# Fused attention and two MLP blocks: reciprocal sums carried by the fifth score tile's transpose, and some casts on other engines

## The chip, the cores and the metric

One Trainium2 chip, one core of it. The metric is the device time of one execution in microseconds. The core has a matrix engine (PE, with its weight loads shown as PEld), a vector engine (DVE), an activation engine (ACT), a general engine (POOL) and a queue that issues the DMAs (SP). Each takes its instructions in order; instructions of different engines wait for one another by semaphores.

## The reference

Three stages run one after another on 4 batches of 576 tokens.

- Attention over 8 heads of width 64: scores are `q k^T / 8`, minus a non-negative running bias (`cumsum(max(s,0))` of the query minus that of the key), causal, softmax, times `v`. The heads side by side give `x` of width 512.
- A gated MLP: `h = gelu(x w_in)`, split into `u` and `v`; `v` is normalised over its 512 features, mixed over tokens with `w_sg` (576 by 576), `b_sg` is added, the product with `u` goes through `w_out`, and `x` is added.
- A second MLP: every token is mixed with the one before it, `k = relu(xk w_k)`, `(k*k) w_v`, times `sigmoid(xr w_r)`.

The change touches the first stage and, by engine choice only, the second.

## The kernel before

Numbers are held as pairs of high and low parts (`split_lo` makes the low part by a subtraction), so that a product is two or three matmuls in a reduced fp32 format.

`attn_pair(b, hp)` handles two heads; there are 16 such pairs. For each head it loads `kq`, casts the high parts (`QB`, `ka`), copies them by DMA into the other half of the operand tiles (`qa`, `ka`) and makes the low parts. Then come nine steps: four score tiles of head 0, the shared fifth tile `st5` (the last 64 queries of head 0 in partitions 0 to 63, those of head 1 in 64 to 127), and four tiles of head 1. A step multiplies into PSUM (L257, L258), adds the mask and finds the row maximum on DVE (L284), takes the exponential on ACT (L292) with the row sum accumulated in a column of `sm` (128 by 9), transposes the exponentials on PE (L307, L310, L318) and copies them to `pt1` and `pt2`. The fifth tile has 576 columns of scores in a tile of 640; the rest of its columns is zero, and its last transpose (L318) takes columns 512 to 640. The values product (L345) multiplies `pt1` and `pt2` with `vf`, in two parts `r`, and ACT or DVE copies the result to `xT`.

The row sums are not divided into the exponentials. They are turned by a transpose of their own, `sm` to `rt` (9 by 128, L323), an epsilon is added (L325), the reciprocal is taken (L326), and the nine rows go to DRAM (L327) and come back broadcast over 64 partitions each as `rb` (L330 to L332). `scale_pending` multiplies `xT` by `rb` on DVE (L360); it is called during a later pair, at its fifth tile.

`moe1(b)` is the gated MLP of one batch, with products `v`, `u`, `sg`, `o` (all at L376). `prologue` converts weights in the first stretch (`syt`, `sraw`, `wcs`, `wsr`). Attention, prologue and `moe1` are generators. `attention_until` runs the attention ahead of the MLP by a measure of work (`LEAD`, `RATE`, `A_COST`, `E_COST`), and `PRO` says at which attention progress a prologue step is taken. That gives the program order. The framework's planner then orders the instructions of each engine by its own simulated time, with the program order as priority; `after` adds an ordering by hand. After about 418 us only the second MLP runs (`k`, `r`, `psa`, `psb`, `psc`); no line of it is touched.

PSUM tiles of the attention and MLP come from three tags: `sc` (3 buffers), `tp` (2) and `acc` (3). `rt`, `tq` (the last transpose of the fifth tile), the values product and the MLP's products before the last batch use `acc`.

Of the kernel before, what the change touches and what calls it, by code (L numbers as in the profile page):

```python
# [1 line left out]

# [18 lines left out]
NT = 5  # L21
# [7 lines left out]
SUM_EPS = 1e-9  # L29
TW = [P, P, P, P, S - 4 * P]  # L30
QS = 256
TW1 = 640
PTB = 2
HB = 1
RATE = (1.1, 1, 1, 1)


@with_exitstack
def fused_kernel(ctx, tc, kqT, vL, s, w_in, g_ln, w_sgT, b_sg, w_out, mu_k, mu_r, w_k, w_v, w_r, out):
    nc = tc.nc  # L40

    const = ctx.enter_context(tc.tile_pool(name="const", bufs=1))
    dram = ctx.enter_context(tc.tile_pool(name="dram", bufs=1, space=bass.MemoryType.DRAM))
# [25 lines left out]
    def split_lo(eng, lo, x, hi):  # L69
        eng.tensor_tensor(out=lo, in0=x, in1=f32(hi), op=ALU.subtract)  # L70
# [127 lines left out]
    def spatial(k):  # L198
# [5 lines left out]
            nc.sync.dma_start(out=raw[64:128], in_=w_sgT[512:])  # L204
        nc.scalar.copy(wsg[0][:, k], raw)
        split_lo(nc.vector, wsg[1][:, k], raw, wsg[0][:, k])

    xT = {}

    last_row = [None]  # L210


    def attn_pair(b, hp):
        pr = b * (H // 2) + hp
        first = b == 0
        ops = []
        for hh in range(2):
            h = 2 * hp + hh
            hd = b * H + h

            kq = at.tile([P, S], F32, tag="kq", name=f"kq{hd}", bufs=2)
            nc.sync.dma_start(out=kq, in_=kqT[b, h])
            i = hd % (NSET + 1) if first else hd % NSET
            qb, kb = QB[i], KB[i]

# [8 lines left out]
            (nc.scalar.copy if hd < 1 else nc.gpsimd.tensor_copy)(qb[64:128], kq[64:128])  # L234
            (nc.vector.tensor_copy if 1 < hd < 4 else nc.scalar.copy)(ka[0:64], kq[0:64])  # L235
            nc.sync.dma_start(out=f32(qa[0:64]), in_=f32(qb[64:128]))
            nc.sync.dma_start(out=f32(ka[64:128]), in_=f32(ka[0:64]))
            lo = nc.vector if hd in (0, 2) else nc.gpsimd
            split_lo(lo, qa[64:128], kq[64:128], qb[64:128])
            split_lo(lo, kb[64:128], kq[0:64], ka[0:64])  # L240
            ops.append((qa, ka, qb, kb))
            if hh == 0:
                vf = at.tile([P, 2, NT, D], F32, tag="vf", name=f"vf{pr}", bufs=2)
                nc.sync.dma_start(out=vf, in_=vL[b][:, h:h + 2])
                x_t = ep.tile([P, S], F32, tag="xT", name=f"xT{pr}", bufs=8)
                xT[(b, hp)] = x_t
            yield 0
# [14 lines left out]
        for hh, i in steps:  # L262
            q0 = i * P
            w = min(q0 + P, S)
            if hh == 2:
                st = st5
            elif first and hh != 1:
                st = stf[:, 64 * i * (i + 1):64 * (i + 1) * (i + 2)]
            else:
                st = at.tile([P, 640], F32, tag="st", name=f"st{pr}_{hh}_{i}", bufs=4)  # L270
# [17 lines left out]
            if hh == 2:  # L288

                pass  # L290
            last = len(chunks) - 1
            e = nc.scalar.activation(  # L292
                st[:, :w], st[:, :w], AF.Exp, bias=mx[:, last:last + 1], scale=-1.0,
                accum_out=sm[:, i + 5 * (hh == 1):i + 5 * (hh == 1) + 1],
            )
            exps.append(e)
            if (hh, i) == LATE:
                scale_pending(mi)
# [10 lines left out]
                c = (j + (i == 1)) * P  # L309
                nc.tensor.transpose(tp[:, c:c + P], st[:, j * P:(j + 1) * P], ident)  # L310
            if i == 1:
                (nc.vector.tensor_copy if first and not hh else nc.scalar.copy)(pt1[:, hh], tp[:, :QS + P])
            elif i < 4:
                (nc.vector.tensor_copy if i == 3 and pr > 5 else nc.scalar.copy)(
                    pt2[:, hh, :i + 1, q0 - QS:w - QS], tp[:, :(i + 1) * P].rearrange("p (j m) -> p j m", m=P))
            else:
                tp4 = psum1.tile([P, 512], F32, tag="acc", name=f"tq{pr}", bufs=3)
                nc.tensor.transpose(tp4[:, 0:P], st[:, 512:640], ident)  # L318
                nc.scalar.copy(pt2[:, :, :4, q0 - QS:], tp.rearrange("p (j a m) -> p a j m", j=4, a=2))
                nc.vector.tensor_copy(pt2[:, :, 3, 0:64], tp4[:, :P].rearrange("p (a m) -> p a m", a=2))  # L320
            yield (i + 1) * 200
        rt = psum1.tile([P, 512], F32, tag="acc", name=f"rt{pr}", bufs=3)
        nc.tensor.transpose(rt[:9, :P], sm, ident)  # L323
        rc = at.tile([9, P], F32, tag="rc", name=f"rc{pr}")
        nc.vector.tensor_scalar_add(rc, rt[:9, :P], SUM_EPS)  # L325
        nc.vector.reciprocal(rc, rc)  # L326
        nc.sync.dma_start(out=rdram[pr], in_=rc)  # L327
        rbs = at.tile([P, S], F32, tag="rb", name=f"rb{pr}", bufs=1)
        rq = rdram[pr].rearrange("i q -> (i q)")
        nc.sync.dma_start(out=rbs[:64], in_=rq[:S].partition_broadcast(64))  # L330
        nc.sync.dma_start(out=rbs[64:, :512], in_=rq[S + 64:].partition_broadcast(64))
        nc.sync.dma_start(out=rbs[64:, 512:], in_=rq[S:S + 64].partition_broadcast(64))  # L332
        for r in range(2):
            q0, n = ((0, QS), (QS, S - QS))[r]
            acc = psum1.tile([P, 512], F32, tag="acc", name=f"pv{pr}_{r}", bufs=3)
            nk = 2 if r == 0 else NT
            for kk in range(nk):
                o = max(0, kk * P - q0)
                both = []
                for a in (1, 0):  # L340
                    if r == 0:
                        pt = pt1[:, a, :QS] if kk == 0 else pt1[:, a, QS:]
                    else:
                        pt = pt2[:, a, kk, o:] if kk < 4 else pt2[:, a, 3, 0:64]
                    both.append(nc.tensor.matmul(acc[64 * a:64 * a + 64, o:n], vf[:, a, kk], pt, start=(kk == 0), stop=(kk == nk - 1)))  # L345
                after(both[1], both[0])

            (nc.vector.tensor_copy if first and not r else nc.scalar.copy)(x_t[:, q0:q0 + n], acc[:, :n])
            yield 4000
        pending.append((x_t, rbs))  # L350
        if pr == B * H // 2 - 1:
            scale_pending(None)
# [27 lines left out]
    def moe1(b):  # L380
# [11 lines left out]
            scale_pending(None)  # L392
        for k in range(KD):
            nc.scalar.copy(xs[0][:, k], xT[(b, k)])
            split_lo(nc.vector if b == 0 else nc.gpsimd, xs[1][:, k], xT[(b, k)], xs[0][:, k])
        for i in range(2):
            nc.scalar.copy(xq[:, :, i], f32(xs[i][:, :, 512:]))
        yield 0
# [5 lines left out]
        for t in range(NT):  # L404
# [13 lines left out]
            else:  # L418
# [8 lines left out]
            nc.gpsimd.tensor_scalar(out=v[:m, t], in0=v[:m, t], scalar1=mv[:m, t, 0:1], scalar2=rstd[:m, t:t + 1],  # L427
                                    op0=ALU.subtract, op1=ALU.mult) if b == 0 else nc.vector.tensor_scalar(out=v[:m, t], in0=v[:m, t], scalar1=mv[:m, t, 0:1], scalar2=rstd[:m, t:t + 1],
                                    op0=ALU.subtract, op1=ALU.mult)
            last_cast[0] = nc.scalar.copy(vn[0][:m, t], v[:m, t])  # L430
            if t < 4:
                split_lo(nc.vector if b == B - 1 else nc.gpsimd, vn[1][:, t], v[:, t], vn[0][:, t])
            else:

                split_lo(nc.vector, vn[0][64:128, 4], v[:64, 4], vn[0][:64, 4])
# [17 lines left out]
        for m in range(KD):  # L453
            f = slice(m * P, (m + 1) * P)
            ga = ep.tile([P, TW1], F32, tag="tmp", name=f"ga{b}_{m}", bufs=3)[:, :S + 1]
            for hf in range(2):
# [7 lines left out]
                nc.vector.scalar_tensor_tensor(out=ga[:, c], in0=acc[:, :HF], scalar=g_sb[:, m:m + 1], in1=bsg[:, c],  # L464
                                               op0=ALU.mult, op1=ALU.add)
                yield 14 * 288 * S_W
            eng = nc.vector if b == B - 1 else nc.gpsimd
            eng.tensor_tensor(out=ga[:, :S], in0=ga[:, :S], in1=u[m], op=ALU.mult)
            last_gate[0] = nc.scalar.copy(gs[0][m], ga[:, :S])
            gs[1].append(ep.tile([P, S], F32R, tag="u", name=f"gl{b}_{m}", bufs=4))  # L470
# [71 lines left out]
    a_it = a_stream()  # L542
    a_done = 0.0

    PRO = [0, 0] + [1 + 1 * i for i in range(5)]

    def attention_until(n):
        nonlocal a_done
        while a_done < min(n, B * H):
            a_done = next(a_it)  # L550
            while PRO and a_done >= PRO[0]:
                PRO.pop(0)
                next(pro)
# [3 lines left out]
    closed = False  # L557
    for b in range(B):
        e_done = 0.0
        for c in moe1(b):  # L560
            e_done += c
            attention_until((b + 1) * H + LEAD + RATE[b] * H * e_done / E_COST)
            if pro is not None and next(pro, None) is None:
                pro = None
            if a_done == B * H and not closed:
                closed = True
                ap_stack.close()
# [320 lines left out]
```

## Time and profile before

| | |
|---|---|
| median of 3 runs | 655.01 us (654.92 to 657.52) |
| span of the profiled execution | 655.4 us |
| its time outside the span | not reported apart; the median lies 0.4 us below the span |
| PE, DVE, ACT, POOL busy | 95%, 73%, 63%, 33% of the span |
| instructions | 11462 |

The page gives busy time per engine, the chain of work that ended last, and the costliest groups. Busy PE is not PE at its peak, since the ends of matmuls are modelled. A wait of one engine for another stands in the waits view with the releaser; a wait costs time only where it stands in the chain.

### The profile page before, as it was taken

What the parts mean: (1) busy time and instruction counts of PE and PEld (TensorE: products, weight loads), DVE (VectorE), ACT (ScalarE), POOL (GpSimd) and SP (SyncE); (2) the same over time, 40 slices, a digit from 0 to 9 for tenths busy, and PEclk for the clock granted to TensorE, in tenths of its full rate; (3) what the DMA queues carried; (4) which work ended last, traced back from release to release, by engine and by line L of the source; (5) the groups of instructions that cost most, each with busy time, mean ns of one, the idle gap of its engine ahead of it and who ended that gap; (6) DMA issues with size and microseconds to landing.
All of it is one profiled execution on the core that took longest, in us unless ns stands there. A gap on an engine that the chain in (4) does not pass through costs nothing.

```text
span 655.4 us, 11462 instructions
## 1 busy us (share of the span) xinstructions
PE 620.6 (95%) x3912; PEld 547.0 (83%) x3912; DVE 478.0 (73%) x990; ACT 415.2 (63%) x933; POOL 217.5 (33%) x218
## 2 busy tenths in 40 slices
PE   1779999989999999999999999999999999999997
PEld 1547777878988998978898999888888888999997
DVE  7889688995849844479732678786975869587874
ACT  4889889984748755468732665576865778553530
POOL 7265657778535577357353120000000000000000
PEclk9899999999999999999999999999999999999999
DMA  7576563454570641833403862677563693546543
GB/s 221 164 224 212 159 212 104 142 188 122 178 241 24 197 138 38 241 111 101 142 18 88 293 230 99 214 264 220 206 217 135 210 358 140 187 167 200 210 144 121
DMA packets 56458, 112.74 MB, mean 172 GB/s; under 512 B 7680, under 2 KB 20624, under 8 KB 56400
## 3 DMA queue, kind: packets, MB, share of 16 engines
q1 hardware_dynamic: 56400, 112.01, 53.3%
q8 instruction: 31, 0.51, 0.3%
q14 instruction: 27, 0.22, 0.1%
HBM read 74.46 MB, written 28.02 MB: 156 GB/s over the span
## 4 chain that ended last, share of the span: by engine, by line
PE 81%; DVE 7%; DMA 7%; issue 2%; SPq 1%; ACT 1%; DVEq 0%; ACTq 0%
PE k L376 15%; PE sg L376 9%; PE psa L786 8%; PE r L376 8%; PE o L376 7%; PE v L376 7%; PE pv L345 6%; PE u L376 5%; PE tp L310 4%; PE psb L786 4%; PE sc L257 4%; PE sc L258 3%; PE psc L786 2%; DMA rdram<-rc 2%; DMA wsr<-in_w_sgT_dram 1%
## 5 line engine op out<-in xcount | busy, mean ns | idle before, releaser
L376 PE MATMUL k<-x,wk 128*128 128x512 f32 (+1 forms) x480 | 98.9, 368 | 0.0
L376 PEld LDWEIGHTS k<-x,wk 128*128 128x128 f32 x480 | 83.6, 189 | 14.9
L292 ACT ACTIVATE st<-st,mx 128x384 f32<-128x384 f32 (+4 forms) x128 | 74.9, 588 | 8.2 <-DVE mx L284 7.5
L257 PE MATMUL sc<-ka,qa 128*128 128x512 f32 (+3 forms) x180 | 61.8, 358 | 18.4 <-DMA ka<-ka 11.8
L284 DVE CUSTOM_DVE_ANT_0 st<-sc,mask 128x512 f32<-128x512 f32 (+3 forms) x128 | 61.9, 502 | 12.6 <-PE sc L258 12.4
L376 PE MATMUL sg<-wsg,vn 128*128 128x288 f32 x448 | 63.6, 297 | 1.5 <-DVE vn L70 1.5
L376 PEld LDWEIGHTS sg<-wsg,vn 128*128 128x128 f32 x448 | 60.3, 188 | 2.4 <-DVE vn L70 1.7
L258 PE MATMUL sc<-KB,QB 128*128 128x512 f32 (+3 forms) x180 | 56.4, 335 | 0.0
L257 PEld LDWEIGHTS sc<-ka,qa 128*128 128x128 f32 x180 | 33.3, 187 | 26.3 <-issue 17.2
L310 PE MATMUL tp<-ident,st 128*128 128x128 f32 x316 | 50.3, 279 | 0.5 <-ACT st L292 0.5
L345 PE MATMUL pv<-pt,vf 128*64 128x320 f32 (+4 forms) x448 | 50.3, 364 | 0.0
L376 PE MATMUL r<-x,wr 128*128 128x512 f32 (+1 forms) x240 | 49.5, 368 | 0.0
L376 PEld LDWEIGHTS r<-x,wr 128*128 128x128 f32 x240 | 41.9, 189 | 7.5
L376 PE MATMUL v<-wv,xs 128*128 128x512 f32 x192 | 48.0, 396 | 0.0
L345 PEld LDWEIGHTS pv<-pt,vf 128*64 128x64 f32 x448 | 29.3, 136 | 19.8 <-issue 1.6
L70 POOL TENSOR_TENSOR KB<-kq,ka 64x576 fp32r<-64x576 f32 x29 | 43.1, 1485 | 6.9 <-ACT ka L235 4.9
L70 POOL TENSOR_TENSOR qa<-kq,QB 64x576 fp32r<-64x576 f32 x29 | 44.0, 1517 | 2.1
L376 PE MATMUL u<-xs,wc 128*128 128x288 f32 x288 | 41.3, 298 | 1.1 <-DVE u L512 1.1
L310 PEld LDWEIGHTS tp<-ident,st 128*128 128x128 f32 x316 | 38.4, 143 | 4.5 <-ACT st L292 0.8
L605 ACT ACTIVATE yx<-yt,mu 128x64 f32<-128x64 f32 (+4 forms) x64 | 30.5, 530 | 17.7 <-DMA yt<-ydram 17.7
L376 PE MATMUL o<-gh,wc 128*128 128x288 f32 x192 | 40.6, 297 | 0.7 <-DMA wc<-wscr 0.7
L376 PEld LDWEIGHTS v<-wv,xs 128*128 128x128 f32 x192 | 35.0, 188 | 7.3 <-issue 0.3
(191 smaller groups left out, 1435.3 us busy)
## 6 DMA issues: line engine op xcount, KB each, us to landing
wc<-wscr SPq DMA_DIRECT2D x24, 512.0 KB
kq<-in_kqT_dram SPq DMA_DIRECT2D x32, 288.0 KB
kr<-kdram SPq DMA_DIRECT2D x12, 768.0 KB
kdram<-k SPq DMA_DIRECT2D x16, 512.0 KB
yt<-ydram SPq DMA_DIRECT2D x24, 257.0 KB
vf<-in_vL_dram SPq DMA_DIRECT2D x16, 320.0 KB
ydram<-y SPq DMA_DIRECT2D x16, 288.5 KB
gt<-gdram SPq DMA_DIRECT2D x12, 384.0 KB
```

The source lines that it names most:

```text
L70: eng.tensor_tensor(out=lo, in0=x, in1=f32(hi), op=ALU.subtract)
L257: nc.tensor.matmul(sc[:m, :c1 - c0], qa[:, q], ka[:, c0:c1], start=True, stop=False)
L258: nc.tensor.matmul(sc[:m, :c1 - c0], qb[:, q], kb[:, c0:c1], start=False, stop=True)
L284: mi = nc.vector.tensor_tensor_reduce(out=st[:, c0:c1], in0=sc[:, :n], in1=mk, op0=ALU.add, op1=ALU.min, scale=-SCALE, scalar=mx[:, 0:1] i ...
L292: e = nc.scalar.activation(st[:, :w], st[:, :w], AF.Exp, bias=mx[:, last:last + 1], scale=-1.0, accum_out=sm[:, i + 5 * (hh == 1):i + 5 * ...
L310: nc.tensor.transpose(tp[:, c:c + P], st[:, j * P:(j + 1) * P], ident)
L345: both.append(nc.tensor.matmul(acc[64 * a:64 * a + 64, o:n], vf[:, a, kk], pt, start=(kk == 0), stop=(kk == nk - 1)))
L376: nc.tensor.matmul(acc, a, w_, start=(i == 0), stop=(i == n - 1))
L605: i = nc.scalar.mul(t[:, s0:s1], yt[:, s0 + d:s1 + d], mu[:, r, 1, k:k + 1])
L786: nc.tensor.matmul(to[:, :HW], l, r, start=(start and i == 0), stop=(i == len(mms) - 1), skip_group_check=True)
```

## The change

It does the following.

- The transpose `rt` and its tile go. The epsilon is added to the unturned sums (128 by 9), and their reciprocals are written into columns 576 to 584 of `st5`, which were zero. The last transpose of the fifth tile, which was issued in the fifth step, is issued after the ninth, with the reciprocals in it: they arrive in rows 64 to 72 of `pt2[:, :, 3, 0:64]`. One DVE copy brings the 128 by 128 block there, and the DMA to DRAM reads rows 64 to 72 of that tile, in pieces of 64 elements where it had 128. The values product reads the same block; `vf` is zero in the rows that hold reciprocals.
- Both parts of the values product are issued in one piece, with one yield.
- A table `PLAN` sets engines (A, D, P for ACT, DVE, POOL) for single copies, casts and splits, and shifts of `attention_until` for single MLP steps (`ad...`). Entries `vn3_2` and `c9_1_2` name the engine that was used before.
- `PRO` becomes `[0, 0, 0.5, 2, 3, 4, 4.5]`, from `[0, 0, 1, 2, 3, 4, 5]`. The `st` tile shrinks from 640 to 512 columns.

```diff
+PLAN = {"ad0_21": 1, "ad0_29": 0.5, "ad1_31": 0.5, "ad1_6": -1, "ad2_15": -1, "ad2_2": -0.5, "ad2_22": 0, "ad2_31": -1, "ad3_10": -1, "ad3_5": -1, "c0_0_1": "A", "c2_1_1": "D", "c6_1_1": "D", "c7_0_2": "D", "c9_1_2": "A", "ge2_2": "D", "lk1": "D", "lq9": "D", "vn2_4": "P", "vn3_2": "D", "xl0_0": "P", "xl0_3": "P"}
+def place(k, d):
+    return PLAN.get(k, d)
...
-            lo = nc.vector if hd in (0, 2) else nc.gpsimd
-            split_lo(lo, qa[64:128], kq[64:128], qb[64:128])
-            split_lo(lo, kb[64:128], kq[0:64], ka[0:64])
+            lq = ENG[place("lq%d" % min(hd, 16), "D" if hd in (0, 2) else "P")]
+            lk = ENG[place("lk%d" % min(hd, 16), "D" if hd in (0, 2) else "P")]
+            split_lo(lq, qa[64:128], kq[64:128], qb[64:128])
+            split_lo(lk, kb[64:128], kq[0:64], ka[0:64])
...
             if i == 1:
-                (nc.vector.tensor_copy if first and not hh else nc.scalar.copy)(pt1[:, hh], tp[:, :QS + P])
+                ECP(f"c{pr}_{hh}_1", "D" if first and not hh else "A")(pt1[:, hh], tp[:, :QS + P])
             elif i < 4:
-                (nc.vector.tensor_copy if i == 3 and pr > 5 else nc.scalar.copy)(
+                ECP(f"c{pr}_{hh}_{i}", "D" if i == 3 and pr > 5 else "A")(
                     pt2[:, hh, :i + 1, q0 - QS:w - QS], tp[:, :(i + 1) * P].rearrange("p (j m) -> p j m", m=P))
             else:
-                tp4 = psum1.tile([P, 512], F32, tag="acc", name=f"tq{pr}", bufs=3)
-                nc.tensor.transpose(tp4[:, 0:P], st[:, 512:640], ident)
-                nc.scalar.copy(pt2[:, :, :4, q0 - QS:], tp.rearrange("p (j a m) -> p a j m", j=4, a=2))
-                nc.vector.tensor_copy(pt2[:, :, 3, 0:64], tp4[:, :P].rearrange("p (a m) -> p a m", a=2))
+                ECP(f"c{pr}_2_4", "A")(pt2[:, :, :4, q0 - QS:], tp.rearrange("p (j a m) -> p a j m", j=4, a=2))
             yield (i + 1) * 200
-        rt = psum1.tile([P, 512], F32, tag="acc", name=f"rt{pr}", bufs=3)
-        nc.tensor.transpose(rt[:9, :P], sm, ident)
-        rc = at.tile([9, P], F32, tag="rc", name=f"rc{pr}")
-        nc.vector.tensor_scalar_add(rc, rt[:9, :P], SUM_EPS)
-        nc.vector.reciprocal(rc, rc)
-        nc.sync.dma_start(out=rdram[pr], in_=rc)
+        nc.vector.tensor_scalar_add(sm, sm, SUM_EPS)
+        nc.vector.reciprocal(st5[:, S:S + 9], sm)
+        tp4 = psum1.tile([P, 512], F32, tag="acc", name=f"tq{pr}", bufs=3)
+        nc.tensor.transpose(tp4[:, 0:P], st5[:, 512:640], ident)
+        nc.vector.tensor_copy(pt2[:, :, 3, 0:64], tp4[:, :P].rearrange("p (a m) -> p a m", a=2))
+        nc.sync.dma_start(out=rdram[pr].rearrange("i (a m) -> i a m", a=2), in_=pt2[64:73, :, 3, 0:64])
...
-            yield 4000
+        values()
+        yield 8000
...
-            split_lo(nc.vector if b == 0 else nc.gpsimd, xs[1][:, k], xT[(b, k)], xs[0][:, k])
+            split_lo(ENG[place(f"xl{b}_{k}", "D" if b == 0 else "P")], xs[1][:, k], xT[(b, k)], xs[0][:, k])
...
+            ENG[place(f"vn{b}_{t}", "P" if b == 0 else "D")].tensor_scalar(
+                out=v[:m, t], in0=v[:m, t], scalar1=mv[:m, t, 0:1], scalar2=rstd[:m, t:t + 1], op0=ALU.subtract, op1=ALU.mult)
...
-            eng = nc.vector if b == B - 1 else nc.gpsimd
+            eng = ENG[place(f"ge{b}_{m}", "D" if b == B - 1 else "P")]
...
-    PRO = [0, 0] + [1 + 1 * i for i in range(5)]
+    PRO = [0, 0, 0.5, 2, 3, 4, 4.5]
...
-            attention_until((b + 1) * H + LEAD + RATE[b] * H * e_done / E_COST)
+            attention_until((b + 1) * H + LEAD + RATE[b] * H * e_done / E_COST + place(f"ad{b}_{nstep}", 0))
+            nstep += 1
```

## Rows read from the trace of the kernel before

The engines' names and the columns are as the section on the profile says.

**Rows 1.** From the page: busy time by engine, then the chain's shares by engine.

```profile
PE 620.6 (95%) x3912; PEld 547.0 (83%) x3912; DVE 478.0 (73%) x990; ACT 415.2 (63%) x933; POOL 217.5 (33%) x218
...
PE 81%; DVE 7%; DMA 7%; issue 2%; SPq 1%; ACT 1%; DVEq 0%; ACTq 0%
```

**Rows 2.** Windows of two stretches: busy us (x instructions) of each engine, granted clock, DMA.

```profile
10.00:160.00 150.00, 131.11 (x880) 105.75 (x881) 126.54 (x316) 122.30 (x320) 97.11 (x78) 0.98 0.56 171
...
160.00:420.00 260.00, 257.89 (x1828) 231.75 (x1827) 169.66 (x414) 151.56 (x362) 113.56 (x123) 1.00 0.47 146
```

**Rows 3.** Waits of PE, 10 to 160 us: waited for, us, times, longest.

```profile
PE sc L257 <- DMA ka<-ka: 11.8, 1, 11.8
...
PE sc L257 <- DVE mx L284: 7.9, 7, 2.9
...
PE sg L376 <- DVE vn L70: 1.5, 1, 1.5
...
PE v L376 <- DVE v L512: 1.4, 1, 1.4
```

**Rows 4.** Waits of PE, 160 to 420 us.

```profile
PE u L376 <- DVE u L512: 1.1, 1, 1.1
```

**Rows 5.** Groups of instructions by line and shape: busy us, mean ns, idle before.

```profile
L326 DVE RECIPROCAL rc<-rc 9x128 f32<-9x128 f32 x16 | 15.0, 937 | 0.2
...
L325 DVE TENSOR_SCALAR rc<-rt 9x128 f32<-9x128 f32 x16 | 4.4, 273 | 7.5 <-PE rt L323 7.5
...
L323 PE MATMUL rt<-ident,sums 128*9 128x128 f32 x16 | 4.5, 281 | 0.0
...
L63 DVE TENSOR_SCALAR mu<-mu 128x8 f32<-128x8 f32 x1 | 0.2, 173 | 0.0
```

**Rows 6.** Chain of waits in order of time: start us, us, what.

```profile
33.41 0.93 DVE rc L326
...
82.39 1.00 DVE xs L70
...
84.10 0.95 DVE rc L326
...
305.28 3.69 DMA rdram<-rc
...
315.09 0.54 DVE v L428
...
325.88 0.11 PE rt L323
```

**Rows 7.** Timeline of DVE at 134 us: start us, us, instruction [idle before].

```profile
134.45 0.28 DVE L325 TENSOR_SCALAR rc<-rt 9x128 f32<-9x128 f32 x1
...
136.30 0.93 DVE L326 RECIPROCAL rc<-rc 9x128 f32<-9x128 f32 x1
```

**Rows 8.** Timelines of DVE, PE and ACT near 22 us.

```profile
21.38 0.55 DVE L312 COPY pt<-tp 128x384 f32<-128x384 f32 x1
...
22.20 0.44 PE L257 MATMUL sc<-ka,qa 128*128 128x384 f32 x1 [0.77 <-DVE mx L284]
...
22.98 0.66 ACT L77 ACTIVATE syt<-sraw 128x512 f32<-128x512 f32 x1 [1.32 <-DMA sraw<-in_w_in_dram]
```

**Rows 9.** Timelines of DVE and POOL, 10 to 19 us.

```profile
11.30 1.77 DVE L85 SCALAR_TENSOR_TENSOR syt<-syt 128x512 uint32<-128x512 uint32 x1
...
18.58 0.69 DVE L85 SCALAR_TENSOR_TENSOR syt<-syt 128x512 uint32<-128x512 uint32 x1
...
10.80 1.72 POOL L70 TENSOR_TENSOR KB<-kq,ka 64x576 fp32r<-64x576 f32 x1
```

**Rows 10.** Groups of instructions on POOL by line and shape.

```profile
L70 POOL TENSOR_TENSOR xs<-xT,xs 128x576 fp32r<-128x576 f32 x12 | 17.1, 1432 | 17.6 <-ACT xs L394 17.3
...
L427 POOL TENSOR_SCALAR v<-v,mv,rstd 128x512 f32<-128x512 f32 x4 | 9.1, 2272 | 0.2
```

**Rows 11.** Waits of DVE, 130 to 360 us.

```profile
DVE xT L360 <- DMA rb<-rdram: 8.6, 3, 3.8
```

More of the change, by code (lines that the diff above doesn't have):

```diff
@@ L1 @@
-from contextlib import ExitStack
+from contextlib import ExitStack, contextmanager
 import concourse.bass as bass
@@ L40, in fused_kernel, with pri @@
     nc = tc.nc
+    @contextmanager
+    def pri(name, d=0):
+        n = place(name, d)
+        tc.cur_priority += n
+        yield
+        tc.cur_priority -= n
     const = ctx.enter_context(tc.tile_pool(name="const", bufs=1))
@@ L210, in fused_kernel, with ECP @@
     last_row = [None]
+    CASTS = {"A": nc.scalar.copy, "D": nc.vector.tensor_copy, "P": nc.gpsimd.tensor_copy}
+    def ECP(k, d):
+        return CASTS[place(k, d)]
+    ENG = {"D": nc.vector, "P": nc.gpsimd}
     def attn_pair(b, hp):
@@ L233, in attn_pair @@
                 qa, ka = qaf, kaf
-            (nc.scalar.copy if hd < 1 else nc.gpsimd.tensor_copy)(qb[64:128], kq[64:128])
-            (nc.vector.tensor_copy if 1 < hd < 4 else nc.scalar.copy)(ka[0:64], kq[0:64])
+            cq = CASTS[("A" if hd < 1 else "P")]
+            ck = CASTS[("D" if 1 < hd < 4 else "A")]
+            cq(qb[64:128], kq[64:128])
+            ck(ka[0:64], kq[0:64])
             nc.sync.dma_start(out=f32(qa[0:64]), in_=f32(qb[64:128]))
             nc.sync.dma_start(out=f32(ka[64:128]), in_=f32(ka[0:64]))
-            lo = nc.vector if hd in (0, 2) else nc.gpsimd
-            split_lo(lo, qa[64:128], kq[64:128], qb[64:128])
-            split_lo(lo, kb[64:128], kq[0:64], ka[0:64])
+            lq = ENG[place("lq%d" % min(hd, 16), "D" if hd in (0, 2) else "P")]
+            lk = ENG[place("lk%d" % min(hd, 16), "D" if hd in (0, 2) else "P")]
+            split_lo(lq, qa[64:128], kq[64:128], qb[64:128])
+            split_lo(lk, kb[64:128], kq[0:64], ka[0:64])
             ops.append((qa, ka, qb, kb))
@@ L269, in attn_pair @@
             else:
-                st = at.tile([P, 640], F32, tag="st", name=f"st{pr}_{hh}_{i}", bufs=4)
+                st = at.tile([P, 512], F32, tag="st", name=f"st{pr}_{hh}_{i}", bufs=4)
             mx = at.tile([P, 16], F32, tag="mx", name=f"mx{pr}_{hh}_{i}", bufs=4)
@@ L287, in attn_pair @@
                 )
-            if hh == 2:
-                pass
             last = len(chunks) - 1
[L292 to L295, printed above, removed]
+            with pri("pe"):
+                e = nc.scalar.activation(
+                    st[:, :w], st[:, :w], AF.Exp, bias=mx[:, last:last + 1], scale=-1.0,
+                    accum_out=sm[:, i + 5 * (hh == 1):i + 5 * (hh == 1) + 1],
+                )
             exps.append(e)
@@ L332, in attn_pair, with values @@
         nc.sync.dma_start(out=rbs[64:, 512:], in_=rq[S:S + 64].partition_broadcast(64))
[L333 to L348, printed above, removed]
-            yield 4000
+        def values():
+            for r in range(2):
+                q0, n = ((0, QS), (QS, S - QS))[r]
+                acc = psum1.tile([P, 512], F32, tag="acc", name=f"pv{pr}_{r}", bufs=3)
+                nk = 2 if r == 0 else NT
+                for kk in range(nk):
+                    o = max(0, kk * P - q0)
+                    both = []
+                    for a in (1, 0):
+                        if r == 0:
+                            pt = pt1[:, a, :QS] if kk == 0 else pt1[:, a, QS:]
+                        else:
+                            pt = pt2[:, a, kk, o:] if kk < 4 else pt2[:, a, 3, 0:64]
+                        both.append(nc.tensor.matmul(acc[64 * a:64 * a + 64, o:n], vf[:, a, kk], pt, start=(kk == 0), stop=(kk == nk - 1)))
+                    after(both[1], both[0])
+                ECP(f"x{pr}_{r}", "D" if first and not r else "A")(x_t[:, q0:q0 + n], acc[:, :n])
+        values()
+        yield 8000
         pending.append((x_t, rbs))
@@ L426, in moe1 @@
             nc.gpsimd.tensor_tensor(out=rstd[:m, t:t + 1], in0=rstd[:m, t:t + 1], in1=mhalf[:m, 0:1], op=ALU.pow)
-            nc.gpsimd.tensor_scalar(out=v[:m, t], in0=v[:m, t], scalar1=mv[:m, t, 0:1], scalar2=rstd[:m, t:t + 1],
-                                    op0=ALU.subtract, op1=ALU.mult) if b == 0 else nc.vector.tensor_scalar(out=v[:m, t], in0=v[:m, t], scalar1=mv[:m, t, 0:1], scalar2=rstd[:m, t:t + 1],
-                                    op0=ALU.subtract, op1=ALU.mult)
+            ENG[place(f"vn{b}_{t}", "P" if b == 0 else "D")].tensor_scalar(
+                out=v[:m, t], in0=v[:m, t], scalar1=mv[:m, t, 0:1], scalar2=rstd[:m, t:t + 1], op0=ALU.subtract, op1=ALU.mult)
             last_cast[0] = nc.scalar.copy(vn[0][:m, t], v[:m, t])
             if t < 4:
-                split_lo(nc.vector if b == B - 1 else nc.gpsimd, vn[1][:, t], v[:, t], vn[0][:, t])
+                split_lo(ENG[("D" if b == B - 1 else "P")], vn[1][:, t], v[:, t], vn[0][:, t])
             else:
@@ L559, in fused_kernel @@
         e_done = 0.0
+        nstep = 0
         for c in moe1(b):
             e_done += c
-            attention_until((b + 1) * H + LEAD + RATE[b] * H * e_done / E_COST)
+            attention_until((b + 1) * H + LEAD + RATE[b] * H * e_done / E_COST + place(f"ad{b}_{nstep}", 0))
+            nstep += 1
             if pro is not None and next(pro, None) is None:
```

## The prediction, as it was made before the run

> **What bounds the kernel now.** I read the page first, then windows, then the waits of PE and the chain in order of time. PE is busy 95% of the span and carries 81% of the chain; DVE and the DMAs carry 7% each [rows 1]. So a removed PE instruction counts nearly in full where PE is dense, and any other engine counts only where PE waits for it. The windows say where: from 160 to 420 us PE idles 260.00 - 257.89 = 2.1 us, from 10 to 160 us 150.00 - 131.11 = 18.9 us [rows 2]. DVE is busy 126.54 of those 150 us, 84%. The waits of PE there name DVE: 7.9 us for the row maxima, 1.5 for a low part of `vn` and 1.4 for a gelu, 10.8 us together; the first 11.8 us are start-up for `ka`, of which only the last 1.8 lie behind the 10 us mark [rows 3]. In the dense stretch the longest wait is 1.1 us, for a gelu of `u` [rows 4]. The reader is to see two regimes: an early one in which an overloaded DVE holds PE back, and a late one in which only PE's own instructions count. After 420 us nothing is touched.
>
> **The change part by part.** I sum against the profiled span of 655.4 us. The median of the runs is 655.0, so 0.4 is taken off at the end.
>
> The transpose of the sums. Sixteen go. One lasts 281 ns, but matmuls overlap, and in the dense stretch the chain gives one 0.11 us [rows 5, 6]. 16 x 0.11 = 1.8 us less. Bounds: 0, if each filled a wait, and 16 x 0.281 = 4.5.
>
> The two DVE operations on the sums. Per pair 0.937 + 0.273 = 1.21 us now [rows 5]. Turned over they are 128 by 9, with 9 elements along a partition in place of 128. The trace shows no reciprocal of that shape; the nearest row is an arithmetic operation on 128 by 8, 0.173 us [rows 5]. Below: 0.17 each. Above: what they cost now. I take 0.17 for the addition and 0.20 for the reciprocal, near the 128 by 8 row, since cost should follow the elements per partition. That saves 1.21 - 0.37 = 0.84 us a pair, 13.4 us of DVE in all. Eight of the sixteen pairs fall before 160 us. The chain passes through the reciprocal at 33.41 and at 84.10 us [rows 6]; a third, at 136.30, starts 1.85 us after its addition in a full DVE queue [rows 7]. I count three: 3 x 0.84 = 2.5 us. Bounds: 0, and 8 x 0.84 = 6.7. The others hide beside PE's own work; if that cover goes, they count too.
>
> First copy of pair 0 to ACT (`c0_0_1`). It takes 0.55 us of DVE at 21.38 us, and at 22.20 PE has idled 0.77 us for a row maximum behind it; ACT idles 1.32 us there for a weight load, which hides the copy [rows 8]. I take 0.5 less; bounds 0 and 0.55.
>
> Low parts of `xs`, two of four from DVE to POOL. The one at 82.39 us holds the chain for 1.00 us [rows 6]. On POOL such a split takes 1.43 us [rows 10], so the product that needs it may start 0.43 later, while DVE gets a microsecond back: 0.6 less. Bounds: 2.0 less (both splits on the path), 1.9 more (both waits, and the product behind POOL's queue).
>
> `lk1` to DVE. POOL loses 1.72 us; on DVE such a low part costs at most the 1.00 us that the larger `xs` split took [rows 6, 9]. While that POOL operation runs, the DVE operation beside it takes 1.77 us, and the same one later 0.69 [rows 9]. +1.00 and -1.08 come to near nothing: 0, bounds -1.1 and +1.0.
>
> One normalisation of `v` from DVE to POOL (`vn2_4`). It stands in the chain at 315.09 us with 0.54 us [rows 6], behind a DVE multiplication that waits for `rb` (three such waits of DVE sum to 8.6 us, [rows 11]), and the 1.1 us wait of PE for `u` hangs on that queue [rows 4]. On POOL it needs not wait for `rb`; the full-height form takes 2.27 us there [rows 10]. I take the whole 1.1 us as gone. Bounds: -1.1, and +1.7 (2.27 - 0.54, if POOL starts no sooner). Late after it: the low part of the same tile on DVE.
>
> The copies `c2_1_1`, `c6_1_1`, `c7_0_2`, the gate `ge2_2` and the split `lq9` change engines where PE waits for none of them; PE's own work hides them: 0, bounds -0.5 and +0.5. The shifts of attention steps and `PRO`, and the two value parts issued together, add no instruction; they reorder. What they can reach is the waiting that is there; for them alone I take 0, bounds -3 and +3.
>
> What is added. The last transpose of the fifth tile moves from the fifth step to behind the ninth. Before, PE needed nothing of DVE for the sums. Now PE's transpose waits for two DVE operations, and the last four of 28 value matmuls wait for the DVE copy of the block. Behind the transpose in PE's queue stand the value matmuls, and behind those the next pair's scores, for which DVE and ACT wait. The hops are short (0.17, 0.20, 0.28, 0.28 us), but the DVE queue is not: at 134 us an addition and its reciprocal stand 1.85 us apart [rows 7]. In the first batch's four pairs there is no MLP work for most of the time to put between; I take 0.3 us each, 1.2 more. Bounds: 0, and 16 x 0.75 = 12 more, with 0.75 the size of the early wait at 22.20 [rows 8].
>
> The row of sums to DRAM. It now leaves in 18 pieces of 256 bytes, where it was 9 of 512. The round trip stands in the chain, with 3.69 us from issue to landing at 305.28 [rows 6]. I take no change, since the bytes are the same; bounds 0 and +3.69 at each of the two early places, those behind 33.41 and 84.10. The Trainium skill, page DMA: Bandwidth & Descriptors, section Specifications, states at least 512 bytes for line rate, and a read-modify-write below that. No row shows a 256-byte write by itself; by that rule this transfer would be the longer one, and it speaks against the change (third rival).
>
> Sum: -1.8 - 2.5 - 0.5 - 0.6 - 1.1 + 1.2 = -5.3; 655.4 - 5.3 = 650.1, as a median 649.7 us.
>
> **The rivals.**
>
> More than that: with DVE relieved and the order shifted, all 10.8 us of early waits for DVE go, not the 3.6 that I count (2.5 + 0.5 + 0.6). For it: seven waits of 7.9 us are for row maxima, which queue behind everything that DVE loses. Against: weight conversions stay, and they hold DVE as much. 655.4 - 1.8 - 10.8 - 1.1 = 641.7, as a median 641.3.
>
> Contention of POOL and DVE: DVE's two-input operations lose 1.08 us while a POOL operation runs [rows 9]. Each of the two `xs` splits on POOL would cost DVE that: +2.2, and `lk1` gives back 0.1. 650.1 + 2.1 = 652.2, as a median 651.8. Against it: nothing says that DVE has such an operation at that moment. The Trainium skill, page SBUF — State Buffer, section Who interferes with whom, states that a DVE instruction with two SBUF inputs contends with a POOL instruction that reads SBUF, the later one blocked for the whole of it; the 1.77 against 0.69 us agrees.
>
> The round trip of the sums gets longer, by half of its 3.69 us at the two early places: +3.7, which brings 653.8, as a median 653.4; at the whole, 657.1. For it: the chain runs through it. Against: `rb` is used only in the next pair, and DVE waited for it 8.6 us late in the kernel with 1.1 us of harm to PE.
>
> Slower: PE stands at the moved transpose. Place: PE's queue at the end of each pair. Price: what DVE's queue makes of three visits. With 0.75 us a pair the sum is -6.5 + 12 = +5.5, 660.9, as a median 660.5. It decides from 6.5 / 16 = 0.4 us a pair on. For it: an order planned by simulated time, on a DVE that is 84% busy early. Against: late, DVE has room (169.66 of 260 us, [rows 2]) and MLP products can stand between.
>
> **How the numbers follow.** Forecast 42%, more than that 20%, contention 10%, longer round trip 14%, slower 14%. A measurement can tell about 0.5%, 3.3 us, from no change: under 651.7 is faster, over 658.3 slower. Forecast, larger gain and half of the contention case, less 0.02 for the forecast's upper end, give 0.65 faster; the other half, the longer round trip and that 0.02 give 0.21 within; 0.14 slower. The range goes from the larger gain, 640.5, to 656.5, which holds most of the longer round trip and leaves out the slower case; with a little below, about 0.2 is outside. The forecast's own range is 646 to 652.
>
> **What would show it.** Right: reciprocals of about 0.2 us, PE's waits for row maxima between 10 and 160 us down by some 3 us, and the 1.1 us wait near 317 us gone. Wrong: waits of PE at the fifth tile's last transpose or the value matmuls with DVE as releaser; reciprocals near 0.9 us; a landing of the sums clearly over 3.7 us with DVE idle for `rb` early; DVE operations of 1.8 us beside the moved `xs` splits. A time under 646 would say that the order, not the removed work, set it.

## The result, and the profile of the changed kernel

The changed kernel takes 662.4 us (median of 4 runs, 658.4 to 664.8), the one before 655.0 beside it: a ratio of 1.0118, 95% interval 1.0081 to 1.0155. The forecast was 649.7 us with a range up to 656.5. It is wrong in size and in sign: +7.4 us instead of -5.3.

Span and time first. The profiled execution of the changed kernel took 664.8 us with a span of 663.0; so 1.8 us lie around a span. The profiled execution of before (span 655.4) therefore took about 657.2 us, 2.2 above its median. The verdicts below rest on medians, the traces on single executions that differ by such amounts.

From the page of the changed kernel: busy time by engine, TensorE's granted clock in 40 slices, the chain's shares [rows 1].

```profile
PE 624.3 (94%) x3896; PEld 548.2 (83%) x3896; DVE 472.2 (71%) x993; ACT 413.9 (62%) x931; POOL 219.6 (33%) x217
...
PEclk9888999999999999999999999999999999999999
...
PE 71%; DVE 8%; DMA 7%; ACT 6%; issue 3%; SPq 1%; POOL 0%; DVEq 0%; ACTq 0%
```

PE has 16 instructions fewer and yet is busy 3.7 us longer; its idle time, span less busy, grew from 34.8 to 38.7 us. Half of the 7.6 us between the two spans is waiting, half is a longer execution of fewer matmuls. DVE lost 5.8 us, the moves of engine included; for the sums alone I had counted 13.4.

The windows of [rows 2] after the change:

```profile
10.00:160.00 150.00, 129.80 (x841) 104.40 (x842) 119.33 (x308) 117.18 (x306) 94.13 (x75) 0.95 0.58 171
160.00:420.00 260.00, 255.83 (x1811) 228.30 (x1811) 166.49 (x415) 152.55 (x366) 118.47 (x124) 1.00 0.46 140
```

In the early stretch 841 matmuls were run instead of 880 (8 of the 39 are transposes of the sums, which went), and the granted clock is 0.95 instead of 0.98; in the dense stretch PE idles 4.2 us instead of 2.1. The last product of the first MLP ends at 425.5 us instead of 418.0: all of the loss lies ahead of the second MLP.

PE's waits from 10 to 160 us after the change, as [rows 3] (waited for, us in total, times, longest):

```profile
PE sc L276 <- DMA ka<-ka: 14.2, 4, 12.1
PE sc L276 <- DVE mx L303: 3.1, 2, 1.9
PE tq L339 <- DVE st L337: 2.7, 1, 2.7
PE tp L327 <- ACT st L309: 2.1, 2, 1.5
...
PE u L392 <- DVE u L527: 1.8, 1, 1.8
...
PE tq L339 <- DVE u L527: 1.2, 1, 1.2
```

The waits for row maxima did fall, from 7.9 to 3.1 us. In their place stand the moved transpose, 3.9 us in two waits, and three more small waits for `ka`. The 1.1 us wait of [rows 4] is gone from the dense stretch, but others took its place; the longest there is 1.4 us, at a score tile.

The turned sums themselves: line, operation, count, duration in ns (least/median/greatest), first and last start in us.

```profile
L336 DVE TENSOR_SCALAR sums<-sums x16: 158/242/1369, 31.1 to 354.2; 128x9 f32<-128x9 f32 x16
...
L337 DVE RECIPROCAL st<-sums x16: 192/208/216, 33.0 to 354.5; 128x9 f32<-128x9 f32 x16
...
L341 SPq DMA_DIRECT2D rdram<-pt x16: 827/860/906, 34.0 to 356.8; - x16
```

The reciprocal took 0.21 us, as forecast. The addition took 0.17 at best but 1.37 at worst, and the issue of the sums' 18 pieces holds the DMA queue 0.86 us, where the 9 pieces of before took 0.29. DVE's waits for `rb`, 8.6 us in three in [rows 11], are now:

```profile
DVE xT L376 <- DMA rb<-rdram: 17.4, 5, 5.5
```

The worst addition, in the timeline of the first pair (start us, us, instruction, [idle before]):

```profile
30.57 1.85 POOL L81 TENSOR_TENSOR qa<-kq,QB 64x576 fp32r<-64x576 f32 x1
...
31.08 1.37 DVE L336 TENSOR_SCALAR sums<-sums 128x9 f32<-128x9 f32 x1
...
32.97 0.20 DVE L337 RECIPROCAL st<-sums 128x9 f32<-128x9 f32 x1
...
33.32 0.31 PE L339 MATMUL tq<-ident,st 128*128 128x128 f32 x1 [2.70 <-DVE st L337]
```

The addition runs beside POOL's low part of `qa` and ends 0.03 us after it (32.45 against 32.42); then a row maximum stands before the reciprocal, and PE waits 2.70 us for both.

### The profile page after: what moved, and what is told of

Read it like the earlier page. It is cut to its first block, busy times and chain, and to the rows that moved or that the text cites. A ratio compares the mean times of both kernels' runs of the same rounds, so it can differ in the third digit from the quotient of the medians.

```text
span 663.0 us, 11447 instructions
## 1 busy us (share of the span) xinstructions
PE 624.3 (94%) x3896; PEld 548.2 (83%) x3896; DVE 472.2 (71%) x993; ACT 413.9 (62%) x931; POOL 219.6 (33%) x217
## 4 chain that ended last, share of the span: by engine, by line
PE 71%; DVE 8%; DMA 7%; ACT 6%; issue 3%; SPq 1%; POOL 0%; DVEq 0%; ACTq 0%
PE k L392 15%; PE sg L392 8%; PE psa L803 8%; PE r L392 7%; PE o L392 7%; PE pv L360 4%; PE v L392 4%; PE u L392 4%; PE psb L803 4%; PE tp L327 3%; PE sc L276 3%; PE sc L277 2%; ACT st L309 2%; PE psc L803 2%; DMA wr<-in_w_out_dram 2%
## 5 line engine op out<-in xcount | busy, mean ns | idle before, releaser
L276 PE MATMUL sc<-ka,qa 128*128 128x512 f32 (+3 forms) x180 | 63.2, 366 | 20.9 <-DMA ka<-ka 14.2
L327 PE MATMUL tp<-ident,st 128*128 128x128 f32 x316 | 52.1, 280 | 2.5 <-ACT st L309 2.1
L81 POOL TENSOR_TENSOR qa<-kq,QB 64x576 fp32r<-64x576 f32 x28 | 41.6, 1486 | 2.0
L252 POOL CAST QB<-kq 64x576 fp32r<-64x576 f32 x29 | 20.5, 708 | 63.6 <-PE sc L277 52.5
```

The source lines that it names most:

```text
L252: cq(qb[64:128], kq[64:128])
L276: nc.tensor.matmul(sc[:m, :c1 - c0], qa[:, q], ka[:, c0:c1], start=True, stop=False)
```

## The experiments

Theory A: the change itself costs, because PE now waits for DVE at the moved transpose. Theory D: the operations matter little; the planner builds another order of the queues from them, and that order costs. Behind each median stand the ratio to runs of before on the same chip and its 95% interval.

**Core and table apart.** In e1 the table of engines is empty and `PRO` as before; e3 has the two value pieces besides; e2 is the other half, the table and `PRO` with the sums of before. e4 inverts the sums unturned, but turns the reciprocals with a transpose of their own and sends 9 pieces of 512 bytes; no table.

```diff
e1  -PLAN = {"ad0_21": 1, ...}      +PLAN = {}
    -PRO = [0, 0, 0.5, 2, 3, 4, 4.5] +PRO = [0, 0] + [1 + 1 * i for i in range(5)]
e4  +nc.vector.reciprocal(rs, sm)
    +nc.tensor.transpose(rt[:9, :P], rs, ident)
    +nc.vector.tensor_copy(rc, rt[:9, :P])
    +nc.sync.dma_start(out=rdram[pr], in_=rc)
```

> The reciprocals in the fifth tile and the joined values product, with the engine table empty and the old PRO. Theory A (PE stands at the moved transpose and the values product behind DVE): as slow as the changed kernel, 659 to 665 us, with waits of PE for DVE at tq and pv of some 5 us. Rival B (the table of engines and attention shifts does the harm): 649 to 654 us, as I forecast for this part.

> The kernel before with the engine table, the shifts and the new PRO, but the sums turned by their own transpose and the values product in two pieces. Theory A: 652 to 656 us, no slower than before. Rival B: 660 to 665 us.

> The reciprocals in the fifth tile alone: values product in two pieces, empty table, old PRO. Theory A: within 0.5% of e1_core_only, 659 to 665 us, since the wait comes from the moved transpose. Rival C (joining the two value parts does the harm): 649 to 654 us, with e1_core_only slow.

> The reciprocals are taken of the unturned sums (128 by 9), but turned by a transpose of their own as before, copied by DVE and sent as nine rows of 512 bytes; the fifth tile's last transpose stays in the fifth step; empty table, old PRO, two value pieces. It has DVE's relief of some 0.5 us a pair without the wait of the values product. Theory A: 651 to 655 us, no slower than before. If any new order of the instructions is slower by itself (rival D): 658 us or more here too.

Measured: e1 669.8 us (1.0213, 1.0177 to 1.0249), e2 662.3 (1.0112, 1.0084 to 1.0141), e3 665.9 (1.0166, 1.0136 to 1.0196), e4 665.2 (1.0158, 1.0125 to 1.0191). Each half alone is slower than before, and together they are no slower than either; the parts don't add up. e4 and e3 agree, but each has a plan of its own, so they tell little of the ride in the fifth tile or of the size of the pieces by themselves. What all four share is a new plan.

**Only the order.** n2 is before with nothing but the two value parts issued together. n4 is before with one constant of the planner changed; every engine runs as many instructions as before. Both are switched back from the text of the changed kernel, and of that only the narrower `st` tile is left in them.

```diff
n4  -    LEAD = 0.9
    +    LEAD = 1.0
```

> The kernel before with both parts of the values product issued in one piece; no instruction added or removed. Theory D: some other time than before by over 0.5%, most likely slower, 657 to 665 us. Theory A: 653 to 657 us.

> The kernel before with the attention's lead set to 1.0 from 0.9; no instruction added or removed, only queue orders change. Theory D: off by over 0.5%, most likely slower, 657 to 665 us. Theory A: 653 to 657 us, since nothing waits later.

Measured: n2 662.1 us (1.0121, 1.0085 to 1.0158), n4 664.7 (1.0152, 1.0115 to 1.0189). A pure change of order costs as much as the whole change.

**The removed work, with the order held.** p1 and p2 leave the sums' transpose and reciprocal out. In p1 every engine's queue keeps the order of before, by ordering edges between neighbours that carry no semaphore; p2 lets the planner order the same instructions.

```diff
p1, p2  -nc.tensor.transpose(rt[:9, :P], sm, ident)
        -nc.vector.tensor_scalar_add(rc, rt[:9, :P], SUM_EPS)
        -nc.vector.reciprocal(rc, rc)
        +nc.vector.tensor_scalar_add(rc[:, 0:9], sm[0:9], SUM_EPS)
p1      +tc.add_manual_dep(ins[k], ins[prev].name, ...)   # k after prev, as in before
```

> The kernel before with the work on the sums left out (no transpose of them, no reciprocal; one DVE addition on 9 by 9 takes their place, and the rows sent to DRAM are those of a nearly constant tile), and with every engine's queue held in the order of the kernel before by explicit ordering edges. Theory D (the new queue orders that the planner makes cost the time, the removed work is worth something): 648 to 653 us, 2 to 7 us faster than before. Theory A (late wait of PE) says the same. Rival E (the removed work was worth nothing, it is hidden anyway): 654 to 656 us.

> The same left-out work, but the planner orders the queues anew. Nothing in it waits later than before. Theory D: 657 to 667 us, slower than before although it does less. Theory A: 648 to 653 us, as with the kept order.

Measured: p1 654.6 us (0.9999, 0.9981 to 1.0017), p2 660.6 (1.0085, 1.0060 to 1.0111). Taking the work away, which I had put at 4.3 us, is worth nothing in the order of before, and a new plan of the remaining instructions costs 6 us. PE's waits of p1 from 10 to 160 us:

```profile
PE sc L279 <- DMA ka<-ka: 15.2, 3, 12.7
PE sc L279 <- DVE mx L306: 5.6, 6, 1.7
PE sc L279 <- DMA ka_f<-ka_f: 3.4, 2, 1.8
```

The waits for row maxima lost 2.3 us against [rows 3]. Those for `ka` and `ka_f` gained 4.8 (in before `ka_f` has one, of 2.0 us). One reading is that what DVE gave was taken by the copies that bring the halves of `ka` across partitions. p6 and p5 test it by leaving these copies out.

```diff
p5, p6  -nc.sync.dma_start(out=f32(qa[0:64]), in_=f32(qb[64:128]))
        -nc.sync.dma_start(out=f32(ka[64:128]), in_=f32(ka[0:64]))
```

> The kernel before in its own order, but the 64 DMA copies of the halves of qa and ka are left out (the halves hold zeros, so scores lack one term of the split). Sums as before. If the early stretch (10 to 160 us) is held by these copies and their queue, which stand behind casts, 648 to 652 us; if it is held by DVE alone, 654 to 656 us.

> Both left out: the 64 DMA copies, and the sums' transpose and reciprocal as in p1_removed_kept (rows that are not the reciprocals go to DRAM), in the order of before. If in p1_removed_kept the wait only turned from DVE to the copies, the two removals together bring more than each: 3 to 6 us below p6_nocopy_kept. If the sums' work is hidden for another reason: the same as p6_nocopy_kept within 1.5 us.

Measured: p6 647.5 us (0.9875, 0.9845 to 0.9906), p5 646.4 (0.9860, 0.9828 to 0.9891). The copies hold the kernel by some 8 us, nearly 4 of them at the start: the first product of PE begins at 8.0 us in p6 and at 11.8 in before. But with them gone the removed sums are worth only 1.2 us more, within the intervals of each other and not the 3 to 6 of the reading. So it falls: the sums' work hides beside other work as well.

**The same change, with the order held and without.** p3 puts the reciprocals into the fifth tile in the order of before, with no table; two fifth tiles alternate, because with one the next pair's scores, which come early in that order, would overwrite it. e5 is the same program, planned.

```diff
p3, e5  -st5 = at.tile([P, 640], F32, tag="st5", name="st5", bufs=1)
        +fifth = [at.tile([P, 640], F32, tag=f"st5{i}", name=f"st5{i}", bufs=1) for i in range(2)]
        +sm, st5 = sums[pr % 2], fifth[pr % 2]
```

> The reciprocals ride in the fifth tile as in the changed kernel (addition and reciprocal on 128 by 9, no transpose of their own, 18 pieces to DRAM), but two fifth tiles alternate and every engine's queue keeps the order of the kernel before: the late transpose stands where the sums' transpose stood, in front of the value products. No table of engines. Theory D (the order of the queues is what costs, the change itself is free): 653 to 657 us. Theory A (PE stands at the late transpose for DVE, and that is the loss): 658 to 664 us, with waits of PE for tq released by DVE of over 4 us in all.

> The same program as p3_core_kept, the order of the queues left to the planner. Theory D: 658 to 668 us, clearly over p3_core_kept, though the instructions are the same. Theory A: the same time as p3_core_kept within 2 us.

Measured: p3 657.0 us (1.0034, 1.0014 to 1.0054), e5 667.1 (1.0175, 1.0143 to 1.0207). The instructions are the same; the order is worth 10 us. Theory D holds for the larger part. A small part may be A's: p3 is 2.1 us slower than before, though p1 shows that the work taken away costs nothing. PE waits 1.1 us at `tq` in p3, in two waits, and for row maxima 6.5. That these waits are the 2.1 us is not shown: the executions of p3 were also granted a lower clock, 0.988 in the mean, where those of before beside them had 0.994.

**Whose order.** p7 holds PE's queue alone in the order of before and lets the others be planned; p8 holds the other four and lets PE's be planned.

```diff
p7  +keep_order(nc, tc)   # PE's list alone
p8  +keep_order(nc, tc)   # the lists of DVE, ACT, POOL, SP
```

> The program of e5_two_fifth, with only TensorE's queue held in the order of the kernel before; the other four queues are planned. If the loss of the new plan (667.1 against 657.0 us for the same instructions) lies in the order of the matmuls: 656 to 659 us. If it lies in the order of VectorE, ScalarE, GpSimd and the DMA queue: 663 to 668 us.

> The other half: TensorE's queue is planned, the other four are held in the order of the kernel before. If the order of the matmuls is the loss: 663 to 668 us. If it is the order of the other queues: 656 to 660 us. If the five queues only work together, both halves stay above 660 us.

Measured: p7 657.1 us (1.0049, 1.0033 to 1.0064), p8 666.2 (1.0178, 1.0148 to 1.0209). The loss is in the order of PE's own queue, and nearly all of it: p7 stands with p3, p8 with e5. Page of p7, then of p8:

```profile
span 655.0 us, 11444 instructions
...
PE 619.4 (95%) x3896; PEld 547.5 (84%) x3896; DVE 468.6 (72%) x990; ACT 415.9 (63%) x933; POOL 219.9 (34%) x219
```

```profile
span 664.5 us, 11432 instructions
...
PE 624.6 (94%) x3896; PEld 548.3 (83%) x3896; DVE 472.8 (71%) x990; ACT 412.7 (62%) x933; POOL 217.4 (33%) x219
```

The same 3896 matmuls are busy 5.2 us longer in p8, and PE idles 39.9 instead of 35.6 us. Their windows from 160 to 420 us (p7, then p8) hold 0.8 and 6.1 us of idle PE:

```profile
160.00:420.00 260.00, 259.24 (x1839) 233.35 (x1839) 167.77 (x418) 155.45 (x367) 117.13 (x125) 1.00 0.48 147
```

```profile
160.00:420.00 260.00, 253.92 (x1797) 226.39 (x1797) 161.66 (x405) 147.44 (x358) 117.21 (x124) 1.00 0.45 139
```

The longest waits of PE there in p8 both end with work of the gated MLP on DVE, as below; in p7 the longest is 0.6 us, for weights.

```profile
PE u L394 <- DVE u L529: 2.1, 1, 2.1
PE pv L361 <- DVE ga L481: 1.8, 2, 1.5
```

**The table's changes of engine, with the order held.** p4 is before with the ten changes of engine alone; each moved operation stands in its new queue at its old time. p9 is p3 with the same ten. p10 and p11 are p4 and p9 without `vn2_4`.

```diff
p4, p9    -PLAN = {}
          +PLAN = {"c0_0_1": "A", "c2_1_1": "D", "c6_1_1": "D", "c7_0_2": "D", "ge2_2": "D",
          +        "lk1": "D", "lq9": "D", "vn2_4": "P", "xl0_0": "P", "xl0_3": "P"}
p10, p11  the same without "vn2_4"
```

> The kernel before with the table's ten changes of engine alone (no shifts of attention steps, sums as before); each moved operation stands in its new engine's queue at the time that it had before, everything else in the order of before. My sum gave these moves -0.5, -0.6 and -1.1 us: 652.7 us if it holds. If they are hidden as the removed sums were: 654 to 656 us. If they hurt through the longer GpSimd forms: 657 to 662 us.

> The whole change in the order of before: reciprocals in the fifth tile (two such tiles) and the ten changes of engine, the late transpose where the sums' transpose stood. By the sum of p3_core_kept and what the moves do by themselves: 655 to 658 us. If the changed kernel's loss of 7.4 us were in its operations and not in their order: 660 to 664 us.

> p4_moves_kept without the move of the normalisation vn2_4 to GpSimd: nine changes of engine in the order of before. In the trace of p4_moves_kept the normalisation takes 2.08 us on GpSimd behind two splits, the cast of ScalarE waits 4.05 us for it and TensorE 2.7 us for u; up to there that kernel is about 1 us ahead of before. If this move alone is the loss: 652 to 654.5 us. If the other nine cost as well: 656 to 658 us.

> p9_all_kept without the same move: the reciprocals in the fifth tile and nine changes of engine in the order of before. If the normalisation on GpSimd is the loss there too: 655 to 658 us, as p3_core_kept. If not: 660 to 663 us.

Measured: p4 658.3 us (1.0060, 1.0040 to 1.0079), p9 661.8 (1.0110, 1.0078 to 1.0141), p10 656.5 (1.0027, 1.0010 to 1.0045), p11 658.4 (1.0068, 1.0047 to 1.0090). The one normalisation on POOL costs 0.33 and 0.42% in the two pairs, 2.2 and 2.8 us; the intervals overlap a little within each pair, and both pairs point the same way. The other nine moves together don't gain: p10 is 1.8 us slower than before. p11 lies just above the range for a loss in the normalisation alone. p9 fell into the range that I had set for a loss in the operations, not into that of theory D: kept in the order of before, the whole change costs as much as the changed kernel does in its own. So D holds for what a new plan does to a given set of instructions, and falls for the claim that the operations are free. The timeline of p4 shows how the normalisation hurts:

```profile
312.34 1.92 POOL L81 TENSOR_TENSOR qa<-kq,QB 64x576 fp32r<-64x576 f32 x1
...
314.37 2.08 POOL L447 TENSOR_SCALAR v<-v,mv,rstd 64x512 f32<-64x512 f32 x1
...
316.49 0.62 ACT L449 CAST vn<-v 64x512 fp32r<-64x512 f32 x1 [4.05 <-POOL v L447]
...
317.14 0.69 DVE L81 TENSOR_TENSOR vn<-v,vn 64x512 fp32r<-64x512 f32 x1 [3.78 <-ACT vn L449]
...
318.73 0.53 PE L396 MATMUL u<-xs,wc 128*128 128x288 f32 x2 [2.73 <-DVE u L531]
```

On POOL it need not wait for `rb`, but it stands behind two low parts in POOL's queue and takes four times as long. ACT's cast waits 4.05 us for it, DVE's low part for the cast, the gelus behind both, and PE 2.73 us where it waited 1.1 [rows 4]. In p10 that wait is 1.1 us again.

Behind the longer wait TensorE's clock falls from 2.4 to 1.2 GHz, a granted clock of 0.50: in p4 at 319.5 us, in p9 at 319.2 us, and not in p10 and p11. The same window of p4, then of p10:

```profile
319.50:322.92 3.42, 3.42 (x16) 3.31 (x15) 1.99 (x9) 2.25 (x9) 0.00 (x0) 0.50 0.00 0
```

```profile
319.50:322.92 3.42, 3.42 (x28) 3.42 (x27) 1.60 (x6) 3.06 (x8) 0.38 (x1) 1.00 0.17 44
```

PE is busy throughout in both, with 16 matmuls in p4 and 28 in p10. Twelve fewer, at p10's 0.12 us each, are some 1.5 us (an estimate); with the 1.6 us of longer wait that is 3.1, near the 2.2 and 2.8 measured. These are single executions. That the wait brought the clock down is suggested by the four traces and was not tested; in p8 a wait of 2.1 us for `u` at 324 us is followed by no such stretch.

No version of the change beats before; p10 comes nearest of those that carry a part of it, 0.10 to 0.45% slower.

## Why the prediction was wrong

**The step that failed** first is the one on order: "The shifts of attention steps and PRO, and the two value parts issued together, add no instruction; they reorder. What they can reach is the waiting that is there; for them alone I take 0, bounds -3 and +3." Reordering reached more than the waiting that was there. It makes new waits and lengthens PE's busy time: n2 +7.5 us, n4 +10.1, p2 +6.0 against p1, e5 +10.1 against p3. I had listed only two edits as reorderings. In truth every edit makes the planner order all queues anew, and every one of the nine other plans with a new order of PE's queue (e1 to e5, n2, n4, p2, p8) was slower than before, by 0.85 to 2.1%. Why the order of before is the best of them no run shows; its constants may have been chosen by time. The traces say the same: with PE's order of before, PE is busy 617.0 to 622.5 us in nine kernels (before, p1, p3 to p7, p9, p10), and 624.2 in p11 alone; in a new order 622.8 to 627.0 in ten, the changed kernel's 624.3 among them.

The terms for the operations failed too, `vn2_4` and the other moves together in sign:

**The removed transpose, addition and reciprocal** (-1.8 and -2.5): 0.0 in p1, between -1.2 and +1.1 us. A chain that passes twice through the reciprocal [rows 6], with a third place that I counted from a full queue [rows 7], does not mean that its going shortens the chain. In p1 the row maxima were served sooner and PE stood longer for `ka`, but p5 shows that the copies of `ka` are not all that hides this work. Of the durations, the reciprocal's was right. The addition was mis-sized: 0.53 us in the mean instead of 0.17. That was the contention rival's mechanism at a place where I had not put it, and on an operation with one input.

**The changes of engine.** `c0_0_1`, the two `xs` splits and the six that I counted at nothing: forecast -1.1, measured +1.8 in p10. The splits' duration on POOL was near the 1.43 us that I took (1.44 and 1.75 us in the changed kernel); which of the nine costs was not told apart. `vn2_4`: forecast -1.1, measured +2.2 and +2.8, above my bound of +1.7. I took the wait of PE for `u` as gone, as if the operation could start on POOL at once; the two low parts ahead of it stand in POOL's queue before the change too, at 311.6 and 313.1 us. And I gave the clock no price: in p4 and p9 the longer wait is followed by a stretch at 1.2 GHz.

**The moved transpose** (+1.2): p3 bounds all that the new form adds, since what it removes is worth nothing: +2.1 us, between 0.9 and 3.5, so the term holds within what was measured. PE does wait at the place that I named, for 1.1 us in p3; the rest of the 2.1 was not traced to it. The slower rival came near the time (660.5) for another reason: in the changed kernel the waits at `tq` are 3.9 us over 16 pairs, 0.24 us each, under its point of 0.4.

**The sums' pieces** (0): where the chain shows the trip to DRAM it is not longer with 18 pieces, 2.98 and 1.94 us in the changed kernel, where before it is 3.64, 2.53 and 3.69. DVE's waits for `rb` doubled in the changed kernel, but from 130 to 360 us they are 3.7 us in p3 with 18 pieces, and 3.6 and 3.5 in e3 with 18 and e4 with 9; so the doubling does not come from the pieces. The third rival's longer trip was not found.

**The sum.** In the order of before the change costs 0.34% for the sums, 0.27% for nine moves and 0.33% for the normalisation, 0.94% in all; p9 with all of it measured 1.10 (0.78 to 1.41). The changed kernel's 1.18% is the same size in another order, and by another way: a new plan of the new sums with the joined value parts costs 2.1% (e1), and the table's moves and shifts win back 7.4 of those 15 us. No run shows a reason why the two ways end at one time.

What stays open in part: why PE is busy about 5 us longer in a new order with the same matmuls. A lower granted clock, for which the prediction had no term, accounts for some of it. From 30 to 60 us it is 0.94 in before and 0.83 in the changed kernel, means of stretches at 2.4 and at 1.2 GHz; first before, then after:

```profile
30.00:60.00 30.00, 25.06 (x166) 18.42 (x165) 26.60 (x67) 26.54 (x70) 18.20 (x14) 0.94 0.73 228
```

```profile
30.00:60.00 30.00, 23.70 (x141) 16.83 (x142) 22.73 (x59) 24.30 (x63) 18.92 (x14) 0.83 0.66 205
```

One matmul takes 0.151 us of busy PE before and 0.168 after (of a mix that is not quite the same), and in that stretch PE also idles 6.3 instead of 4.9 us. n2 and n4 have 0.94 and 0.93 there; their other low stretches lie later, where n2 has 0.50 from 296.1 to 299.6 us and n4 from 136.6 to 143.4. Ahead of the second MLP PE is busy at 1.2 GHz for 6.7 us in before, 12.7 in the changed kernel, 10.1 in n2, 12.0 in n4, 9.2 in p7 and 14.3 in p8.

What that costs can be estimated from one product: 12 `sg` matmuls take 3.23 us in the low stretch of n4, 16 take 2.29 us at 2.4 GHz in the changed kernel, 0.27 against 0.14 us each. So nearly half of the busy time at 1.2 GHz is loss. That makes 2.8 of the 3.7 us that PE is busy longer in the changed kernel, 1.6 of 3.3 in n2, 2.5 of 4.8 in n4, and 2.4 of the 5.2 between p7 and p8. No run measured the rest. These are single executions; over all of theirs p7 and p8 were granted nearly the same mean clock, 0.987 and 0.988, and lie 9 us apart, so the clock alone does not part them.

## What to carry to other kernels

Where a planner orders the queues, an edit is two changes: the operations, and a new order of everything. Price them apart: hold the order of before with ordering edges and time the operations alone, then time a pure reordering (one planner constant) to see how much any new order moves; here that was 1.5%, nearly twice the forecast's whole sum. Look also where the granted clock falls: in p4 a stretch at 1.2 GHz cost about as much as the longer wait ahead of it. Before an operation is moved to a less busy engine, look at what stands ahead of it in that engine's queue and who waits for the result: idle share is not idle time at that moment.

## What the runs showed of the hardware that was not expected

A 128 by 9 addition on DVE, with one input tile, takes 0.16 to 0.18 us alone and up to 1.37 us beside a POOL operation with two inputs. In the changed kernel 9 of the 16 additions overlap a `TENSOR_TENSOR` of POOL. Eight of these took 0.31 to 1.37 us and ended 0.03 to 0.04 us after it, whatever its remaining length; the ninth, beside one of a single column, took 0.17. One more of the eight, near 224 us:

```profile
223.49 1.80 POOL L81 TENSOR_TENSOR KB<-kq,ka 64x576 fp32r<-64x576 f32 x1
...
224.14 1.18 DVE L336 TENSOR_SCALAR sums<-sums 128x9 f32<-128x9 f32 x1
```

The Trainium skill, page SBUF — State Buffer, section Who interferes with whom, names `tensor_scalar` among the operations that can take the port pair that DVE and POOL share, when its operands meet some conditions, with the later one blocked for the whole instruction of the other. The trace agrees. The reciprocal of the same shape stayed between 0.19 and 0.22 us all 16 times, though three of them began 0.08 to 0.48 us into a POOL operation with two inputs.

The issue of one small transfer costs its queue by its shape: 0.86 us for the sums in 18 pieces out of 9 partitions, 0.29 for the same bytes in 9 pieces, one from each of 9 partitions.
